# Layer norm up to six tiles ahead, spreads issued in the turning step, six weight pieces behind the MLP's first block, kh ahead of weight copies

## The chip, the core and the metric

The kernel runs on one core of a Trainium2 chip. The metric is the time of one execution on the device in microseconds (us), as the median of several runs. A profiled execution gives the trace: every instruction of the engines PE (TensorE: matmuls and transposes; PEld is its weight load), DVE (VectorE), ACT (ScalarE), POOL (GpSimd) and of SP (SyncE), whose queue issues all DMAs here. Each engine and SP's queue take their instructions strictly in the program's order, so whatever stands behind a waiting instruction on the same engine waits too.

## The reference

Two layers, each of a linear attention block and an MLP, both with a residual, on x of 2048 rows by 448 columns in float32:

```python
x = A_x
x = x + _A_ref(_layernorm(x), A_wqkv, A_wo)     # layer 0
x = x + _B_ref(_layernorm(x), B_w1, B_b1, B_w2, B_b2)
...                                             # the same two lines again: layer 1
def _A_ref(x, wqkv, wo):
    q, k, v = ...                               # x @ wqkv, 16 heads of 28
    pq, pk = phi(q), phi(k)                     # phi(t) = where(t > 0, t + 1, exp(t)) + 1e-6
    kv = einsum("bhsd,bhse->bhde", pk, v)
    z = einsum("bhsd->bhd", pk)
    num = einsum("bhqd,bhde->bhqe", pq, kv)
    den = einsum("bhqd,bhd->bhq", pq, z)[..., None] + 1e-6
    return (num / den) @ wo                     # heads put side by side again
def _B_ref(x, w1, b1, w2, b2):                  # w1: 448 x 1792, w2: 1792 x 448
    return gelu(x @ w1 + b1) @ w2 + b2
```

## The kernel before

The 2048 rows are 16 tiles of 128 rows. A float32 product is made from three matmuls on rounded pieces (hi x hi, hi x lo, lo x hi), so every operand is split: ACT casts the high piece, DVE or POOL subtracts it to get the low one. That holds for activations (`XH`, `XL`), for kh and kl, for the normalized tile (`xnh`, `xnl`), for q's and k's weights, and for w1 and w2.

**Phase 1** (`phase1`, L456) goes over the tiles in steps t = 0 to 15. In step t it does, for tile t: K (PE, 11 matmuls with k's weights into `psk`), kp (ACT and DVE: phi), kh (ACT casts kh, L400, DVE subtracts to kl and adds e to `za`, which becomes z), s (ACT and POOL split the normalized tile), G (PE, 11 matmuls of the *previous* tile's xn with its kh and kl, into the four banks `acc`), Q (PE, 11 matmuls with q's weights; steps 0 to 9 only, six Q blocks are kept as fill for later) and, one step later, qp (phi of q and its store to DRAM). For later tiles it does a (LN statistics: `bn_stats`, `bn_aggr`, an add on DVE, then `rs`, a power on POOL), n (DVE normalizes in place), and tu (DVE turns 32 x 32 squares into `sq`; every second tile the pair is stored to DRAM by SP, L257). sp (SP, four DMAs, L263) reads the pair back spread out, so that it is transposed; X splits it to XH and XL for K. The first six tiles of layer 0 are transposed on PE instead (T, L228, with a small ACT copy `tail` of the last columns). In the source G is thus a tile behind K: PE's order is K(t), T(t+1), G(t-1), Q(t), K(t+1).

The order inside a step is the string `STEP` (L447). Tile t + 4 is normalized in step t, with four exceptions in `FIRST` (L448), and an x tile is loaded two steps ahead of that. Layer 1's tiles 0 to 3 are normalized, turned and spread in the last MLP block of layer 0.

**Weights of the MLP** are staged in 30 pieces (`bg_pieces`, L296): 16 of w1, 14 of w2. `background(n)` (L324) first works off the pieces it asked for last time (ACT casts, POOL subtracts), then asks for n more: SP issues the load into one of two buffers tagged `xn`, so an issue waits until POOL is done with the piece two before. Phase 1 of layer 0 calls it with `BG = 2` in steps 1 to 15, between tu and kh; two more calls after phase 1 work off the rest.

**Between phase 1 and the MLP** stands a list in `ORDER` (L439): the last G, z (PE, then ACT's `zb`, L512), gt (ACT and DVE copy the four banks), kv (PE, L533), the mask, four products with wo (`m`), the first four tiles' output, with the six Q blocks as fill. wv and wo come from `trans_load` (L500), called at t = 14.

**The MLP** runs over four blocks b of 512 rows, in each over 14 columns i of 128 of the 1792: `mlp1` of column i + 1 (11 matmuls into `hp`, ACT's gelu `g` and cast `gh`, DVE's `gl`), work for the next block's attention (`behind`, in the order of the `PLAN` tables), `mlp2` of column i (12 matmuls). SP's DMAs before the first block copy M's pieces to new rows (`trans_chunks`, L565).

The x tiles share nine buffers (`H`), `sq`, `sp`, wv and wo share five (`S`).

Of the kernel before, what the change touches and what calls it, by code (L numbers as in the profile page):

```python
# [22 lines left out]
def linear_attn_mlp_kernel(  # L23
# [15 lines left out]
    S, D = x0.shape  # L39
# [31 lines left out]
    def t512(tag, bufs, name, dt=F32):  # L71
        return work.tile([128, 512], dt, name=name, tag=tag, bufs=bufs)
# [15 lines left out]
    def stage_piece(src, c, eng, s):  # L88

        if c < 3:  # L90
            eng.dma_start(s, src[c * 128:(c + 1) * 128, :])
        else:
            eng.dma_start(s[0:64], src[TL:D, :])
            eng.dma_start(s[64:128], src[TL:D, :])
        return s
# [198 lines left out]


    def bg_pieces():  # L296
        for fc in range(4):
            sl = slice(fc * D, (fc + 1) * D)
            for c in range(4):
                s = stage_piece(w1[:, sl], c, sp, t512("xn", 2, "stg")[:, :D])  # L300

                def go(c=c, s=s, sl=sl):
                    if c < 3:
                        act.copy(w1h[:, c, sl], s)
                        pool.tensor_tensor(w1l[:, c, sl], s, f(w1h[:, c, sl]), op=OP.subtract)
                    else:
                        tmp = t512("e", 3, "bx", F32R)[:, :D]
                        act.copy(tmp, s)
                        act.copy(w1x[0:64, sl], s[0:64])
                        pool.tensor_tensor(w1x[64:128, sl], s[64:128], f(tmp[64:128]), op=OP.subtract)  # L310
                yield go
        for i in range(NF):
            s = t512("xn", 2, "stg")[:, :D]
            sp.dma_start(s, w2[i * 128:(i + 1) * 128, :])

            def go(i=i, s=s):
                act.copy(w2h[:, i], s)
                pool.tensor_tensor(w2l[:, i], s, f(w2h[:, i]), op=OP.subtract)
            yield go
# [4 lines left out]
    def background(n):  # L324
        while bg_wait:
            bg_wait.pop(0)()
        for _ in range(n):
            g = next(bg, None)
            if g is not None:
                bg_wait.append(g)  # L330
# [28 lines left out]
    def stage_sp(l, t):  # L359
        if t >= TURNED[l]:  # L360
            block(("a", l, t // 4))
            spread(("a", l, t // 4), t % 4 // 2)
# [28 lines left out]
        ke[l, t] = phi(o, "ek", o)  # L391

    ke = {}
    BG = 2

    def stage_kh(l, t, za):
        e = ke.pop((l, t))
# [46 lines left out]
    )  # L444
    DEFER = NT - ORDER.split().count("Q")

    STEP = "sp a qp K T X s n G kp tu bg kh Q"  # L447
    FIRST = {0: (2, 3), 1: (4,), 2: (5, 6), 3: (7,)}  # L448
    loaded = {0: 3}

    def load_to(l, t):
        for u in range(loaded.get(l, 0), min(t + 1, NT)):
            load_x(l, u)
        loaded[l] = max(loaded.get(l, 0), min(t + 1, NT))

    def phase1(l, tr):  # L456
        za = consts.tile([128, D], F32, name="za", tag="za")
        acc = [bank("acc", 4, f"G{c}")[:, :D] for c in range(4)]
        for t in range(NT):
            load_to(l, (4 if l == 0 else 5) if t == 0 else t + 6)  # L460
            norm = [u for u in (FIRST.get(t, (t + 4,)) if l == 0 else (t + 4,)) if u < NT]
            for tok in STEP.split():
                if tok == "sp":
                    if (t + 3) % 2 and t + 3 < NT and (l == 0 or t >= 2):
                        stage_sp(l, t + 3)
                elif tok == "a":
                    for u in norm:
                        stage_a(l, u)
                elif tok == "n":
                    for u in norm:  # L470
                        stage_n(l, u)
                elif tok == "tu":
                    for u in norm:
                        stage_t(l, u)
                elif tok == "T" and t + 1 < NT:
                    stage_b(l, t + 1)
                elif tok == "X" and t + 1 < NT and (l == 0 or t + 1 >= 4):
                    stage_x(l, t + 1)
                elif tok == "K":
                    stage_k(l, t)  # L480
                elif tok == "qp":
                    stage_qphi()
                elif tok == "kp":
                    stage_kphi(l, t)
                elif tok == "kh":
                    stage_kh(l, t, za)
                elif tok == "s":
                    stage_s(l, t)
                elif tok == "G" and t >= 1:
                    stage_g(l, t - 1, acc)  # L490
                elif tok == "bg" and l == 0 and t >= 1:
                    background(BG)
                elif tok == "Q" and t < DEFER:
                    stage_q(l, t)
            if t == 14:
                trans_load(l, tr)
        return za, acc


    def trans_load(l, tr):  # L500
        tr.wv = stage_square(wqkv[:, 2 * D:])
        tr.wo = []
        for h in range(2):
            s = half("wot")[:G, :2 * D].rearrange("p (g n) -> p g n", g=2)
            sp.dma_start(s, wo[h * 2 * G:(h + 1) * 2 * G, :].rearrange("(g p) n -> p g n", p=G))
            tr.wo += [s[:, 0], s[:, 1]]
# [73 lines left out]
        sp.dma_start(pqt[l, t], pq_d[l][t * 128:(t + 1) * 128, :])  # L580

    def q_z(l, b, j, tr):
        pz = pzs[l, b, j] = t448(f"W{4 + j % 2}", 1, "pz")
        pool.tensor_tensor(pz, pqt[l, b * 4 + j], tr.zb, op=OP.mult)  # L584

    def q_scale(l, b, j, tr):
# [215 lines left out]
    for l in range(LAYERS):  # L802
        tr = SimpleNamespace(mp={})
        za, acc = phase1(l, tr)
        if l == 0:
            background(99)
            background(0)
        fill = list(range(DEFER, NT))

# [20 lines left out]
        for b in range(NB):  # L830
            acc = [bank("acc", 4, f"y{j}")[:, :D] for j in range(4)]
            nxt = b + 1 < NB
            if not nxt and l + 1 < LAYERS:
                st_k = stage_square(wqkv[:, D:2 * D])
                st_q = stage_square(wqkv[:, :D])
                load_to(l + 1, 3)
            for i in range(NF):
                if i + 1 < NF:
                    mlp1(l, b, i + 1)
                elif nxt:  # L840
                    mlp1(l, b + 1, 0)
                if nxt:
                    behind(l, b, i, tr)
                elif l + 1 < LAYERS:
                    if i == 2:
                        split_kq("k", st_k)
                    if i == 5:
                        split_kq("q", st_q)
                    if i in (3, 4, 6, 7):
                        t = (3, 4, 6, 7).index(i)  # L850
                        stage_a(l + 1, t)
                        stage_n(l + 1, t)
                        stage_t(l + 1, t)
                    if i in (6, 9):
                        stage_sp(l + 1, 1 if i == 6 else 3)
                    if i >= 9 and i < 13:
                        stage_x(l + 1, i - 9)
                mlp2(l, b, i, acc)

# [27 lines left out]
```

## Time and profile before

| what | value |
|---|---|
| time, median of 3 runs (lowest to highest) | 910.58 us (910.14 to 912.22) |
| the profiled execution's own time | 911.72 us |
| its span, first to last instruction | 910.0 us |
| mean granted PE clock | 0.991 |
| idle time of PE before G's first matmul, waiting for kh (L400), five times | 5.2 us |
| idle time of PE before the first kv matmul, waiting for gt | 2.0 us |

In rows in order of time the first number is the start in us from the span's start, the second the length; the engine, line and operation follow, then output<-inputs. A bracket at the end tells how long the engine had been idle and what ended that. In rows of stretches the first pair is the stretch; a number in (x...) counts instructions, those that the edge cuts among them; the last three numbers are the granted PE clock (1.00 is full speed), the DMA engines' busy share and GB/s. Matmuls are pipelined and overlap in the rows, so PE can be shown busy and still be held up. SPq is SP's DMA queue.

### The profile page before, as it was taken

What the parts mean: (1) busy time and instruction counts of PE and PEld (TensorE: products, weight loads), DVE (VectorE), ACT (ScalarE), POOL (GpSimd) and SP (SyncE); (2) the same over time, 40 slices, a digit from 0 to 9 for tenths busy, and PEclk for the clock granted to TensorE, in tenths of its full rate; (3) what the DMA queues carried; (4) which work ended last, traced back from release to release, by engine and by line L of the source; (5) the groups of instructions that cost most, each with busy time, mean ns of one, the idle gap of its engine ahead of it and who ended that gap; (6) DMA issues with size and microseconds to landing.
All of it is one profiled execution on the core that took longest, in us unless ns stands there. A gap on an engine that the chain in (4) does not pass through costs nothing.

```text
span 910.0 us, 11659 instructions
## 1 busy us (share of the span) xinstructions
PE 885.5 (97%) x4184; PEld 777.0 (85%) x4184; DVE 498.1 (55%) x970; ACT 340.0 (37%) x586; POOL 207.2 (23%) x243
## 2 busy tenths in 40 slices
PE   7999879999999999999999999999999999999998
PEld 5899768888888888888889998888888888888887
DVE  5798548645744735225448885865555654433112
ACT  3677633422322332333345554342233132222222
POOL 4466742213113102002013233230220220210000
PEclk8999989999999999999999999999999999999999
DMA  6386460532324231132124436145124134020001
GB/s 172 106 239 207 138 197 28 174 105 90 120 87 132 71 104 47 47 118 78 60 81 152 152 110 184 51 123 162 57 76 165 57 115 136 24 70 15 26 1 41
DMA packets 62762, 93.71 MB, mean 103 GB/s; under 512 B 8816, under 2 KB 57968, under 8 KB 62704
## 3 DMA queue, kind: packets, MB, share of 16 engines
q1 hardware_dynamic: 62704, 92.97, 33.1%
q8 instruction: 33, 0.54, 0.3%
q14 instruction: 25, 0.20, 0.1%
HBM read 55.65 MB, written 34.08 MB: 99 GB/s over the span
## 4 chain that ended last, share of the span: by engine, by line
PE 75%; DVE 7%; issue 1%; ACT 1%; DMA 1%; POOL 0%; SPq 0%; DVEq 0%; POOLq 0%
PE y L699 10%; PE y L701 9%; PE y L700 9%; PE hp L683 8%; PE hp L682 8%; PE hp L681 8%; PE hp L685 3%; PE hp L684 3%; PE op L634 2%; PE op L633 2%; PE op L635 2%; PE psq L279 1%; PE psq L280 1%; PE psq L281 1%; PE G L428 1%
## 5 line engine op out<-in xcount | busy, mean ns | idle before, releaser
L691 DVE TENSOR_TENSOR gl<-g,gh 128x512 fp32r<-128x512 f32 x112 | 78.4, 700 | 311.8 <-ACT gh L690 311.8
L687 ACT ACTIVATE g<-hp,b1s 128x512 f32<-128x512 f32 x112 | 77.1, 688 | 410.7 <-PE hp L685 410.6
L699 PE MATMUL y<-w2h,gh 128*128 128x448 f32 x448 | 163.8, 366 | 0.6 <-DVE x L705 0.6
L701 PE MATMUL y<-w2h,gl 128*128 128x448 f32 x448 | 163.7, 365 | 0.0
L700 PE MATMUL y<-w2l,gh 128*128 128x448 f32 x448 | 163.6, 365 | 0.0
L683 PE MATMUL hp<-XL,w1h 128*128 128x512 f32 x336 | 131.3, 391 | 0.3 <-DVE XL L270 0.3
L681 PE MATMUL hp<-XH,w1h 128*128 128x512 f32 x336 | 131.5, 391 | 0.1
L682 PE MATMUL hp<-XH,w1l 128*128 128x512 f32 x336 | 131.5, 391 | 0.0
L183 POOL TENSOR_TENSOR brs<-bve,mhalf 128x1 f32<-128x1 f32 x64 | 40.1, 627 | 385.2 <-DVE bve L181 379.8
L699 PEld LDWEIGHTS y<-w2h,gh 128*128 128x128 f32 x448 | 84.1, 188 | 10.3 <-issue 1.4
L700 PEld LDWEIGHTS y<-w2l,gh 128*128 128x128 f32 x448 | 84.1, 188 | 8.3
L701 PEld LDWEIGHTS y<-w2h,gl 128*128 128x128 f32 x448 | 84.2, 188 | 6.6
L683 PEld LDWEIGHTS hp<-XL,w1h 128*128 128x128 f32 x336 | 63.1, 188 | 14.7 <-DVE XL L270 1.2
L681 PEld LDWEIGHTS hp<-XH,w1h 128*128 128x128 f32 x336 | 63.1, 188 | 11.7 <-ACT XH L269 0.8
L682 PEld LDWEIGHTS hp<-XH,w1l 128*128 128x128 f32 x336 | 63.1, 188 | 11.3
L690 ACT CAST gh<-g 128x512 fp32r<-128x512 f32 x112 | 69.7, 622 | 3.6
L584 POOL TENSOR_TENSOR pz<-pq,zb 128x448 f32<-128x448 f32 x32 | 37.3, 1174 | 82.0 <-DVE dn L590 46.9
L177 DVE BATCH_NORM_STATS2 bst<-x 128x6 f32<-128x448 f32 x64 | 39.9, 623 | 7.6 <-DMA x<-in_A_x_dram 3.4
L648 POOL TENSOR_TENSOR x<-x,b2b 128x448 f32<-128x448 f32 x32 | 36.8, 1150 | 31.6 <-DVE xm L190 23.3
L684 PE MATMUL hp<-XH,w1x 128*128 128x512 f32 x112 | 43.6, 389 | 0.0
L685 PE MATMUL hp<-XL,w1x 128*128 128x512 f32 x112 | 43.6, 389 | 0.0
L427 PE MATMUL G<-kh,xnh 128*128 128x448 f32 x96 | 37.1, 386 | 5.2 <-ACT kh L400 5.2
(144 smaller groups left out, 1584.2 us busy)
## 6 DMA issues: line engine op xcount, KB each, us to landing
x<-in_A_x_dram SPq DMA_DIRECT2D x32, 224.0 KB, 3.8
pq_d<-eq SPq DMA_DIRECT2D x32, 224.0 KB, 2.3
pq<-pq_d SPq DMA_DIRECT2D x32, 224.0 KB, 3.4
x<-x_d SPq DMA_DIRECT2D x32, 224.0 KB, 3.6
sq_a<-sq SPq DMA_DIRECT2D x13, 512.0 KB, 2.9
sp<-sq_a SPq DMA_DIRECT2D x52, 128.0 KB, 3.1
sq_q<-sq SPq DMA_DIRECT2D x12, 512.0 KB, 2.6
sp<-sq_q SPq DMA_DIRECT2D x48, 128.0 KB, 3.0
```

What stands on the lines that cost most here:

```text
L183: pool.tensor_tensor(rs, ve, mhalf, op=OP.pow)
L681: pe.matmul(o, w1h[:, c, s], x.moving(x.hi, c), start=(c == 0), stop=False)
L682: pe.matmul(o, w1l[:, c, s], x.moving(x.hi, c), start=False, stop=False)
L683: pe.matmul(o, w1h[:, c, s], x.moving(x.lo, c), start=False, stop=False)
L684: pe.matmul(o, w1x[:, s], x.moving(x.hi, 3), start=False, stop=False)
L685: pe.matmul(o, w1x[:, s], x.moving(x.lo, 3), start=False, stop=True)
L687: act.activation(g, hp, AF.Gelu_apprx_tanh, bias=b1s[:, i:i + 1])
L690: act.copy(gh, g)
L691: dve.tensor_sub(gl, g, f(gh))
L699: pe.matmul(acc[j], gh[:, s], w2h[:, i], start=first, stop=False)
L700: pe.matmul(acc[j], gh[:, s], w2l[:, i], start=False, stop=False)
L701: pe.matmul(acc[j], gl[:, s], w2h[:, i], start=False, stop=last)
```

## The change

- LN runs further ahead. `NORM` lists for each layer and step which tiles are normalized; in layer 0 all are done by step 9 (before: step 11), in layer 1 by step 8; some steps take two tiles. Loads follow it. Layer 1's tile 4 joins tiles 0 to 3 in the last MLP block (`PRE`).
- sp is the last token of the step that turns the odd tile, no longer the first of a later one.
- Step 0 has an order of its own, `STEP_0`: kp stands ahead of a, s and kh.
- In all steps kh stands ahead of bg.
- `BG` is a list: two pieces per step in steps 1 to 9, one in steps 10 to 15, 24 in all. The last six go through two other buffers (tags W5 and W6) and are asked for in columns 0 to 5 of the MLP's first block of layer 0, each worked off one column later. So that W5 is free, the blocks after the first use W4 alone for pz.
- wv is loaded after step 11 and wo after step 13 (both after step 14 before).

The lines that this text speaks of:

```diff
+        def stage():
+            nonlocal n
+            n += 1
+            if n <= LATE:
+                return t512("xn", 2, "stg")[:, :D]
+            return t448(f"W{5 + n % 2}", 1, "stg")
...
-    BG = 2
...
-    STEP = "sp a qp K T X s n G kp tu bg kh Q"
-    FIRST = {0: (2, 3), 1: (4,), 2: (5, 6), 3: (7,)}
+    STEP = "a qp K T X s n G kp tu kh bg Q sp"
+    STEP_0 = "K T X kp a s kh n tu G Q bg sp"
+    NORM = (
+        ((2,), (3, 4), (5, 6), (7,), (8,), (9,), (10, 11), (12,), (13, 14), (15,)),
+        ((5,), (6,), (7,), (8,), (9, 10), (11,), (12,), (13, 14), (15,)),
+    )
+    PRE = 5
+    BG = [0] + [2] * 9 + [1] * 6
+    LATE = sum(BG)
...
-            load_to(l, (4 if l == 0 else 5) if t == 0 else t + 6)
-            norm = [u for u in (FIRST.get(t, (t + 4,)) if l == 0 else (t + 4,)) if u < NT]
-            for tok in STEP.split():
+            norm = NORM[l][t] if t < len(NORM[l]) else ()
+            if t + 1 < len(NORM[l]):
+                load_to(l, min(NORM[l][t + 1][-1] + 1, NT - 1))
+            for tok in (STEP if t else STEP_0).split():
                 if tok == "sp":
-                    if (t + 3) % 2 and t + 3 < NT and (l == 0 or t >= 2):
-                        stage_sp(l, t + 3)
+                    for u in norm:
+                        if u % 2:
+                            stage_sp(l, u)
...
-                elif tok == "bg" and l == 0 and t >= 1:
-                    background(BG)
+                elif tok == "bg" and l == 0:
+                    background(BG[t])
...
-            if t == 14:
+            if t == 11:
+                tr.wv = stage_square(wqkv[:, 2 * D:])
+            if t == 13:
                 trans_load(l, tr)
...
-        pz = pzs[l, b, j] = t448(f"W{4 + j % 2}", 1, "pz")
+        pz = pzs[l, b, j] = t448(f"W{4 if b else 4 + j % 2}", 1, "pz")
...
-            background(99)
             background(0)
...
+                if l == 0 and b == 0:
+                    background(1)
```

Three places show the order on an engine. First ACT in layer 0, from the split of tile 12 (`xnh`, the first operation of step 12 here) to the split of tile 13's XH; `ek` and `kh` are phi and the cast of k, `w2h` the cast of a weight piece. Before:

```order
L379 CAST xnh<-x_12_717 128x448
L289 ACTIVATE ek<-psk 128x448
L290 ACTIVATE ek<-ek 128x448
L317 CAST w2h<-stg 128x448 x2
L400 ACTIVATE kh<-psk,tiny 128x448
L269 CAST XH<-sp 128x512
```

And in the changed kernel:

```order
L388 CAST xnh<-x_12_638 128x448
L289 ACTIVATE ek<-psk 128x448
L290 ACTIVATE ek<-ek 128x448
L408 ACTIVATE kh<-psk,tiny 128x448
L326 CAST w2h<-stg 128x448
L269 CAST XH<-sp 128x512
```

kh has moved ahead of the weight casts, and there is one cast instead of two; the next XH still stands behind it.

Second, DVE in layer 0, step 0, from its first instruction after the weights' splits (tile 1's XL is L235; L177 to L181 are a tile's LN statistics, L347 or L356 its normalization, L292 on `psk` is k's phi). Before:

```order
L177 BN_STATS bst<-x_2_92 128x6
L179 BN_AGGR bmv<-bst 128x2
L181 TENSOR_SCALAR bve<-bmv 128x1
L177 BN_STATS bst<-x_3_211 128x6
L179 BN_AGGR bmv<-bst 128x2
L181 TENSOR_SCALAR bve<-bmv 128x1
L235 TENSOR_TENSOR XL<-tp,XH 128x512
L347 TENSOR_SCALAR x_2_92<-x_2_92,bmv,brs 128x448
L347 TENSOR_SCALAR x_3_211<-x_3_211,bmv,brs 128x448
L292 SCALAR_TENSOR_TENSOR psk<-psk,ek 128x448
L401 SCALAR_TENSOR_TENSOR kl<-psk,kh 128x448
L403 COPY za<-psk 128x448
```

And in the changed kernel:

```order
L235 TENSOR_TENSOR XL<-tp,XH 128x512
L292 SCALAR_TENSOR_TENSOR psk<-psk,ek 128x448
L177 BN_STATS bst<-x_2_92 128x6
L179 BN_AGGR bmv<-bst 128x2
L181 TENSOR_SCALAR bve<-bmv 128x1
L409 SCALAR_TENSOR_TENSOR kl<-psk,kh 128x448
L411 COPY za<-psk 128x448
L356 TENSOR_SCALAR x_2_92<-x_2_92,bmv,brs 128x448
```

XL and psk now come first, tile 3 has moved out of the step, and tile 2's normalization stands behind kl and za.

Third, SP's queue at the end of phase 1 in layer 0. L257 stores the last pair of turned tiles, L263 spreads it, L314 or L323 loads a piece of w2, L114 to L118 load wv, L505 or L523 load wo. Before:

```order
L257 DMA sq_a_3_1_1165<-sq 128x1024
L314 DMA stg<-in_B_w_dram 128x448 x2
L263 DMA sp<-sq_a_3_1_1165 32x4x256 x4
L314 DMA stg<-in_B_w_dram 128x448 x6
L114 DMA stg<-in_A_wqkv_dram 128x2x448
L116 DMA stg<-in_A_wqkv_dram 128x448
L117 DMA stg<-in_A_wqkv_dram 64x448
L118 DMA stg<-in_A_wqkv_dram 64x448
L505 DMA wot<-in_A_wo_dram 112x2x448 x2
L314 DMA stg<-in_B_w_dram 128x448 x2
```

And in the changed kernel:

```order
L257 DMA sq_a_3_1_1052<-sq 128x1024
L323 DMA stg<-in_B_w_dram 128x448 x2
L263 DMA sp<-sq_a_3_1_1052 32x4x256 x4
L427 DMA pq_d_71<-eq 128x448
L323 DMA stg<-in_B_w_dram 128x448 x2
L114 DMA stg<-in_A_wqkv_dram 128x2x448
L116 DMA stg<-in_A_wqkv_dram 128x448
L117 DMA stg<-in_A_wqkv_dram 64x448
L118 DMA stg<-in_A_wqkv_dram 64x448
L323 DMA stg<-in_B_w_dram 128x448 x2
L523 DMA wot<-in_A_wo_dram 112x2x448 x2
L323 DMA stg<-in_B_w_dram 128x448 x2
```

Ten pieces were loaded after the last store, six of them in a row ahead of wv; now there are eight, two at a time: ahead of the spread, ahead of wv, between wv and wo, and behind wo. (L427 is the store of the last eq, which stood further up.)

More of the change, by code (lines that the diff above doesn't have):

```diff
@@ L296, in bg_pieces @@
     def bg_pieces():
+        n = 0
+        def stage():
[4 more added lines that the diff above has]
+            return t448(f"W{5 + n % 2}", 1, "stg")
         for fc in range(4):
@@ L299, in bg_pieces @@
             for c in range(4):
-                s = stage_piece(w1[:, sl], c, sp, t512("xn", 2, "stg")[:, :D])
+                s = stage_piece(w1[:, sl], c, sp, stage())
                 def go(c=c, s=s, sl=sl):
@@ L312, in bg_pieces @@
         for i in range(NF):
-            s = t512("xn", 2, "stg")[:, :D]
+            s = stage()
             sp.dma_start(s, w2[i * 128:(i + 1) * 128, :])
@@ L445, in linear_attn_mlp_kernel @@
     DEFER = NT - ORDER.split().count("Q")
-    STEP = "sp a qp K T X s n G kp tu bg kh Q"
-    FIRST = {0: (2, 3), 1: (4,), 2: (5, 6), 3: (7,)}
+    STEP = "a qp K T X s n G kp tu kh bg Q sp"
[7 more added lines that the diff above has]
+    LATE = sum(BG)
     loaded = {0: 3}
     def load_to(l, t):
-        for u in range(loaded.get(l, 0), min(t + 1, NT)):
+        for u in range(loaded.get(l, 0), t + 1):
             load_x(l, u)
-        loaded[l] = max(loaded.get(l, 0), min(t + 1, NT))
+        loaded[l] = max(loaded.get(l, 0), t + 1)
     def phase1(l, tr):
@@ L500, in trans_load @@
     def trans_load(l, tr):
-        tr.wv = stage_square(wqkv[:, 2 * D:])
         tr.wo = []
@@ L835, in linear_attn_mlp_kernel @@
                 st_q = stage_square(wqkv[:, :D])
-                load_to(l + 1, 3)
+                load_to(l + 1, PRE - 1)
             for i in range(NF):
@@ L848, in linear_attn_mlp_kernel @@
                         split_kq("q", st_q)
-                    if i in (3, 4, 6, 7):
-                        t = (3, 4, 6, 7).index(i)
+                    if i in (3, 4, 6, 7, 8):
+                        t = (3, 4, 6, 7, 8).index(i)
                         stage_a(l + 1, t)
@@ L853, in linear_attn_mlp_kernel @@
                         stage_t(l + 1, t)
-                    if i in (6, 9):
-                        stage_sp(l + 1, 1 if i == 6 else 3)
-                    if i >= 9 and i < 13:
+                        if t % 2:
+                            stage_sp(l + 1, t)
+                    if 9 <= i < 13:
                         stage_x(l + 1, i - 9)
```

## The prediction

> **What bounds the kernel now.** I read the page's first part, then the busy times by stretch, then the rows in order of time where a stretch loses something. On the page, engine PE (TensorE's matmuls) is busy almost all the time:
> ```profile
> PE 885.5 (97%) x4184; PEld 777.0 (85%) x4184; DVE 498.1 (55%) x970; ACT 340.0 (37%) x586; POOL 207.2 (23%) x243
> ```
> So only PE's lost time can be won. The next view cuts the span where PE changes its work; the columns are length, then each engine's busy time (and instructions), the granted PE clock, DMA share and GB/s.
> ```profile
> 17.41:36.77 19.36, 15.54 (x76) 13.20 (x75) 14.09 (x31) 9.16 (x20) 7.19 (x11) 1.00 0.19 62
> 69.00:92.00 23.00, 23.00 (x115) 21.32 (x114) 19.40 (x41) 17.15 (x34) 15.12 (x18) 1.00 0.71 211
> 92.09:118.28 26.19, 23.54 (x98) 19.06 (x97) 12.40 (x21) 16.12 (x31) 19.36 (x21) 0.93 0.51 150
> 120.12:161.85 41.73, 36.43 (x189) 30.86 (x188) 29.96 (x62) 14.15 (x27) 13.53 (x14) 0.96 0.30 93
> 466.65:482.02 15.37, 13.85 (x59) 12.16 (x58) 11.03 (x24) 6.58 (x11) 3.89 (x6) 0.89 0.47 162
> 482.02:547.60 65.58, 65.58 (x324) 60.57 (x323) 55.03 (x107) 38.65 (x71) 21.85 (x31) 1.00 0.45 141
> 547.60:566.17 18.57, 17.48 (x82) 14.97 (x82) 9.69 (x15) 8.24 (x16) 5.15 (x8) 1.00 0.72 186
> 566.17:601.38 35.21, 34.26 (x189) 29.50 (x189) 29.13 (x62) 13.31 (x25) 11.87 (x12) 1.00 0.14 50
> ```
> Row 482.02 has PE busy throughout: 65.58 over 324 is 0.2024 us per matmul. Matmuls overlap, so a stretch's loss is its length less its count times that, not its idle time.
> - Layer 0, steps 0 to 2 (17.41): 66 matmuls of 448 columns (76 less 8 transposes at about 0.11 and two cut by the edge) need 14.2; lost 5.1.
> - Layer 0, steps 10 to 15 (92.09): 97 x 0.2024 = 19.6; lost 6.6.
> - The stage between phase 1 and the MLP holds the same 189 instructions in both layers: 41.73 in layer 0, 35.21 in layer 1; lost 6.5.
> - Layer 1, start (466.65): 58 x 0.2024 = 11.7; lost 3.6.
> - Layer 1, last steps (547.60): 81 x 0.2024 = 16.4; lost 2.2.
>
> Together 24.0 us: the most that this change can win. Part of it is a halved clock, seen in equal stretches of 3.41 us (first and second of each pair adjacent):
> ```profile
> 111.45:114.87 3.42, 1.75 (x7) 1.00 0.27 72
> 114.87:118.28 3.41, 3.41 (x10) 0.50 0.90 297
> 473.27:476.68 3.41, 1.89 (x9) 1.00 0.00 0
> 476.68:480.09 3.41, 3.41 (x11) 0.50 0.17 67
> 22.71:26.12 3.41, 1.87 (x8) 1.00 0.00 0
> 26.12:29.53 3.41, 3.41 (x19) 1.00 0.43 133
> ```
> A stretch with PE busy for 1.75 or 1.89 us was followed by one at 0.50, which costs 1.7; one with 1.87 was not. About 1.5 us of idle time in one such stretch is the edge. The kv stage holds a third (its clock is 0.96 over 41.73). The Trainium skill ("TensorE: Matmul & The Clock Gate", section on HAM oscillation) lets the clock fall only after a PE gap of over some 3.4 us; these rows contradict it. By that rule the forecast below would be 897.8.
>
> **Kh ahead of the weight copies; one piece per step; six pieces later (layer 0, steps 10 to 15).** In order of time, ACT, the PE matmul behind it, and the same pattern after phase 1:
> ```profile
> 112.38 0.56 ACT L317 CAST w2h<-stg 128x448 fp32r<-128x448 f32 x1 [2.29 <-DMA stg<-in_B_w_dram]
> 112.85 0.63 ACT L400 ACTIVATE kh<-psk,tiny 128x448 fp32r<-128x448 f32 x1
> 113.53 0.47 PE L427 MATMUL G<-kh,xnh 128*128 128x448 f32 x1 [1.49 <-ACT kh L400]
> 125.34 1.12 ACT L317 CAST w2h<-stg 128x448 fp32r<-128x448 f32 x2 [7.48 <-DMA stg<-in_B_w_dram]
> 127.47 0.45 PE L533 MATMUL kvp<-gt,stg 128*112 128x112 f32 x2 [1.99 <-ACT gt L523]
> ```
> ACT waits for a weight's DMA, kh stands behind it, PE behind kh. The DMA is late because of SP's queue:
> ```profile
> 101.10 13.42 SPq L314 DMA_DIRECT2D stg<-in_B_w_dram  x6
> 114.57 0.43 SPq L114 DMA_DIRECT2D stg<-in_A_wqkv_dram  x1
> 117.88 1.04 SPq L314 DMA_DIRECT2D stg<-in_B_w_dram  x2
> ```
> Six issues crawl for 13.42 us, each waiting for one of two buffers; wv and wo wait behind them, and the last two pieces behind those. Afterwards kh waits only for psk, and a late copy holds only the next XH, which PE wants a K block and a G block later (22 matmuls, 4.5 us). With LN done by step 9, DVE drops out too. I leave 0.3 for kl and take 0.4 for step 8 (below): **-5.9**; bounds -4.0 (copies still hold XH once or twice) and -6.5.
>
> **The kv stage.** With one piece per step, wv at step 11 and wo at step 13, the last two copies still stand ahead of zb on ACT, but their DMAs are issued one step apart instead of after 13.42 us of crawl. PE has G(14), a Q block, zp and G(15) to do meanwhile, over 33 matmuls or 6.7 us. Layer 1, without copies, is the nearest row: 35.21. I take nearly all of the 6.5: **-6.3**; bounds -4.5 and -6.5.
>
> **Six pieces behind the MLP's first block.** The price is not the six casts (ACT idles 3.60 per column below) but the first one's wait:
> ```profile
> x<-in_A_x_dram SPq DMA_DIRECT2D x32, 224.0 KB, 3.8
> ```
> That is the page's median landing time for a load of a piece's size; then in order of time:
> ```profile
> 175.71 0.59 SPq L565 DMA_DIRECT2D wq<-Ml  x1
> 176.95 0.69 ACT L687 ACTIVATE g<-hp,b1s 128x512 f32<-128x512 f32 x1 [3.60 <-PE hp L685]
> 181.89 0.69 ACT L687 ACTIVATE g<-hp,b1s 128x512 f32<-128x512 f32 x1 [3.60 <-PE hp L685]
> ```
> The first piece's DMA comes behind the 14 chunk copies, so it is issued at 176.3 in these times and lands near 180. Its cast stands ahead of the g of 176.95, which would start near 180.5; g and gh take ACT 1.34 (4.94 per column less 3.60), to 181.9, gl follows. PE uses gh from about 181.8, when its next hp is done. **+0.4**, between 0 and 1.5. Later pieces are issued a column (4.94) or more ahead. SP's spread of sq_q moves by some 2 us; its reader comes two columns later. POOL's pz now waits for DVE's read of the one buffer, which comes just before it anyway: nothing.
>
> **Layer 0, steps 0 to 2.** What PE waited for:
> ```profile
> 17.06 0.63 DVE L177 BATCH_NORM_STATS2 bst<-x 128x6 f32<-128x448 f32 x1
> 18.01 0.62 DVE L177 BATCH_NORM_STATS2 bst<-x 128x6 f32<-128x448 f32 x1
> 18.95 0.68 DVE L235 TENSOR_TENSOR XL<-tp,XH 128x512 fp32r<-128x512 f32 x1
> 19.55 1.63 DVE L347 TENSOR_SCALAR x<-x,bmv,brs 128x448 f32<-128x448 f32 x2
> 19.69 0.47 PE L281 MATMUL psk<-wk,XL 128*128 128x448 f32 x1 [1.52 <-DVE XL L235]
> 22.65 0.63 DVE L292 SCALAR_TENSOR_TENSOR psk<-psk,ek 128x448 f32<-128x448 f32 x1 [1.48 <-ACT ek L290]
> 24.07 0.47 PE L427 MATMUL G<-kh,xnh 128*128 128x448 f32 x1 [1.82 <-ACT kh L400]
> ```
> Two tiles' statistics (0.95 each, 18.01 to 18.95) stood ahead of XL and psk. Now XL and psk go first: from 17.06, XL 0.68, psk 0.63, one tile's statistics 0.95, kl and za like psk about 0.6 each, normalizing 0.8 (half of 1.63), and a small ACT copy, some 0.3, end near 21.6. Only then can PE transpose tile 2. It was through K(1) nine matmuls after the wait at 19.69; without that wait (1.52 and some 0.16 of overlap) this is 19.69 - 1.68 + 1.8 = 19.8. So 1.8 is lost there (a halved clock after it, 1.7 more, is in the bound), but G then finds kh ready. Steps 1 and 2 norm two tiles each, so DVE stays behind: adding up the same durations, I find 0.4 at G(1)'s kl and 1.0 at the Q block whose bank eq must free first. 3.2 of 5.1 stays: **-1.9**; bounds -0.5 and -4.0.
>
> **Two tiles in one step** (layer 0 steps 6 and 8, layer 1 steps 4 and 7). DVE's groups between 40 and 90 us:
> ```profile
> L347 DVE TENSOR_SCALAR x<-x,bmv,brs 128x448 f32<-128x448 f32 x8 | 9.0, 1129 | 0.0
> L251 DVE STREAM_TRANSPOSE sq<-x 128x384 f32<-128x384 f32 x8 | 4.5, 564 | 0.0
> ```
> A step with Q is 33 matmuls, 6.7 us; DVE is busy 19.40 of 23.00 there, 5.6 per step. One more tile adds 0.95 + 1.13 + 0.56 + some 0.3 = 2.9, so 8.5: 1.8 over. But G(t) comes 6.7 after K(t) and the chain from ek to kl needs about 3.1 (1.3 from psk's start to kh's end in layer 1's rows below, and three more instructions of 0.6), so DVE may run late by 1.8 once; between steps 6 and 8 it regains only about one. I take 0 at step 6 and the 0.4 above at step 8. Spreads, SP and loads: a spread in the turning step only moves ahead of one x load, and that tile is needed a step later.
>
> **Layer 1, start and end.**
> ```profile
> 470.61 0.63 DVE L177 BATCH_NORM_STATS2 bst<-x 128x6 f32<-128x448 f32 x1 [3.14 <-DMA x<-x_d]
> 473.49 0.62 DVE L292 SCALAR_TENSOR_TENSOR psk<-psk,ek 128x448 f32<-128x448 f32 x1
> 472.31 1.01 POOL L380 TENSOR_TENSOR xnl<-x,xnh 128x384 fp32r<-128x384 f32 x1
> 474.83 0.47 PE L427 MATMUL G<-kh,xnh 128*128 128x448 f32 x1 [1.33 <-ACT kh L400]
> ```
> psk will now go before the new tile, at about 471.6, so kh is ready when PE ends K(1) (474.83 - 1.33 - 0.16 = 473.34). What is late next: on POOL, xnl of tile 0 stands behind the rs of the new tile. Here xnl ended 2.7 after that tile's statistics began (470.61 to 473.32); begun at 472.2, behind psk, that is 474.9, where PE wants it at 473.75, with G's third matmul. 1.3 with its overlap stays and, being under 1.5, most likely brings no halved clock: **-2.3**; bounds -0.8 and -3.6. At the end the spreads leave steps earlier and 0.3 stays: **-1.9**; bounds -1.0 and -2.2.
>
> **The rivals.**
> - *DVE sets the pace in the two-tile steps.* If no slack hides them, 4 x 1.8 = 7.2 comes back: 899.9. For it: DVE's 19.40 of 23.00. Against: the row at 482.02, where it is busy 55.03 of 65.58 and PE never waits. 0.07.
> - *The halved clock has another cause than these stalls.* Then three half-clock stretches stay, 3 x 1.7 = 5.1: 897.8. Against it: each fall comes right after a stretch that was half idle. 0.05. This is what the Trainium skill's rule above would give.
> - *zb still waits for the last two copies*, so the change does not do this part: the kv stage keeps its 6.3: 899.0. 0.07.
> - *Slower: casts hold ACT in the MLP block.* If each of the six waited the 7.48 seen at 125.34, a column would take ACT 7.48 + 0.56 + 1.34 (its busy time per column, 4.94 - 3.60) = 9.4 instead of 4.94; six times 4.4, less a slack of 3.5 (gh ends near 178.3, 1.34 after g's start, and is needed at 181.8), is 23: about 915. It decides against the change from 6.7 of wait per cast. Against it: SP has nothing of that length queued there. 0.09, of which 0.03 ends within 0.2%.
>
> **How the numbers follow.** -5.9 - 6.3 + 0.4 - 1.9 - 2.3 - 1.9 = -17.9. The profiled execution took 911.72, 1.72 around a span of 910.0, and lies 1.14 over the median of the runs, 910.58. From its own time the sum gives 893.8; from the median, which I predict, 892.7. The ends of all terms give gains of 22.8 and 9.3, so 887.8 to 901.3, which takes in the three mild rivals. Forecast 0.72. A measurement of this kernel tells about 0.2% (1.8 us) from no change: faster 0.91, same 0.03, slower 0.06.
>
> **What would show it.** Right: no PE wait for kh after 40 us; the stage from zp to the first hp near 35.4 in layer 0; the clock at half only around the start. Wrong step by step: PE waiting for the tp transpose by far more than 1.7 near 20 us; for kl in steps 6 or 8; for y's gh in the MLP's first columns; for xnl at layer 1's first G by over 1.3. The forecast as a whole falls if steps 10 to 15 still take more than 4.5 each.

## The result, and the profile after

The changed kernel takes 896.01 us (median of 4 runs, 895.77 to 896.46) against 911.4 for the kernel before beside it. That is 15.4 us less; the ratio is 0.9829 (95% interval 0.9808 to 0.985). 892.7 was forecast, with a range of 887.8 to 901.3. Of the 3.3 us between forecast and result, 0.8 is the kernel before itself: its median was 910.58 when the forecast was made and is 911.4 with one more run. The profiled execution spans 894.7 (before 910.0). The page's first part:

```profile
PE 878.8 (98%) x4184; PEld 772.8 (86%) x4184; DVE 502.3 (56%) x970; ACT 339.5 (38%) x586; POOL 209.1 (23%) x243
```

PE issues the same 4184 instructions in the same order in both kernels, so a stage can be cut at the start of the *same* matmul in both. Here are the stretches of the kernel before, cut that way at K(12), zp, the first and sixth hp, the first y of block 1 and K(2) and K(13) of layer 1 (length, then each engine's busy time and instructions, granted clock, DMA share, GB/s):

```profile
93.51:120.12 26.61, 23.96 (x100) 19.45 (x99) 12.19 (x21) 15.12 (x29) 18.21 (x20) 0.94 0.54 154
161.85:184.12 22.27, 22.27 (x105) 19.34 (x103) 12.77 (x26) 8.96 (x13) 4.99 (x4) 1.00 0.62 191
184.12:246.21 62.09, 61.58 (x286) 53.20 (x285) 35.14 (x72) 17.53 (x29) 11.70 (x12) 1.00 0.27 88
481.41:548.43 67.02, 67.02 (x331) 61.90 (x330) 56.41 (x110) 39.08 (x71) 22.64 (x32) 1.00 0.45 142
```

And of the changed one:

```profile
91.61:111.68 20.07, 20.07 (x101) 18.60 (x100) 12.19 (x18) 13.95 (x27) 13.93 (x17) 1.00 0.64 188
111.68:147.34 35.66, 34.44 (x189) 29.40 (x188) 29.88 (x62) 13.32 (x25) 12.43 (x13) 1.00 0.18 62
147.34:170.40 23.06, 22.54 (x104) 19.26 (x103) 11.83 (x22) 10.46 (x16) 7.69 (x7) 1.00 0.67 209
170.40:233.09 62.69, 61.64 (x286) 53.20 (x285) 39.24 (x76) 19.55 (x33) 17.00 (x16) 1.00 0.33 103
453.53:465.95 12.42, 11.76 (x57) 10.25 (x55) 7.97 (x17) 5.99 (x10) 3.90 (x6) 1.00 0.48 169
465.95:534.15 68.20, 68.20 (x332) 61.94 (x330) 55.47 (x109) 39.76 (x73) 21.59 (x31) 1.00 0.52 166
534.15:550.06 15.91, 15.91 (x78) 14.45 (x77) 9.37 (x13) 8.16 (x15) 4.78 (x6) 1.00 0.32 100
550.06:585.50 35.44, 34.41 (x189) 29.42 (x188) 29.70 (x62) 13.31 (x25) 11.48 (x12) 1.00 0.14 48
```

From K(12) to zp PE no longer stops at all: 20.07 busy of 20.07. The stage after it is down to layer 1's length. Here are the rows on which the argument rests from the changed kernel's view of what PE waits for (total, times, longest):

```profile
PE psk L279 <- ACT XH L234: 3.1, 1, 3.1
PE y L717 <- ACT g L705: 1.7, 2, 0.9
PE tp L228 <- DVE x L356: 1.2, 1, 1.2
PE G L437 <- POOL xnl L389: 0.7, 1, 0.7
PE y L719 <- DVE gl L709: 0.5, 1, 0.5
PE psq L279 <- DVE eq L292: 0.5, 1, 0.5
PE G L436 <- DVE kl L409: 0.4, 1, 0.4
```

No row for kh is left, the kv stage (zp to the first hp) is within 0.3 of the foretold 35.4, and the clock is at half only around the start and at the very end, as the prediction wanted it. Its last sign was a limit of 4.5 for each of steps 10 to 15: they take 4.46, but for step 11 with 4.72. The next table has the stage lengths of all the kernels that the argument needs, cut at the same matmuls (us, each the difference of two starts in the profile). "Weights alone" and the like are experiments below.

| kernel | Q(1) to K(12) | K(12) to zp | zp to 1st hp | 1st to 6th hp | to block 1's y | layer 1: K(0) to K(2) | K(2) to K(13) | K(13) to zp |
|---|---|---|---|---|---|---|---|---|
| before | 66.65 | 26.61 | 41.73 | 22.27 | 62.09 | 14.76 | 67.02 | 17.76 |
| changed | 67.66 | 20.06 | 35.67 | 23.06 | 62.69 | 12.42 | 68.20 | 15.91 |
| changed, again | 66.96 | 20.06 | 35.72 | 23.37 | 62.67 | 12.34 | 66.88 | 15.61 |
| kh alone | 66.66 | 26.76 | 43.76 | 22.27 | 62.11 | 13.26 | 67.03 | 18.41 |
| weights alone | 67.60 | 28.47 | 35.84 | 24.10 | 62.68 | 13.32 | 67.02 | 21.98 |
| weights, wv late | 66.64 | 22.92 | 39.39 | 23.33 | 62.83 | 13.23 | 68.15 | 17.29 |
| layer norm alone | 68.26 | 22.16 | 42.16 | 22.26 | 62.10 | 12.41 | 68.20 | 15.91 |
| best | 66.72 | 20.06 | 35.76 | 22.27 | 62.10 | 11.49 | 68.20 | 15.91 |

By this table and the 2.9 won before Q(1) (26.86 to 23.95), the 15.3 us between the two spans are: -2.9, +1.0, -6.5, -6.1, +0.8, +0.6, -2.3, +1.2, -1.9, and +0.8 in the rest. Three of these stages held a half-clock stretch in the kernel before's trace (K(12) to zp, the kv stage, layer 1's K(0) to K(2)) and hold none now, so about 5 of the 15.3 are clock and the others are waits.

### The profile page after: what moved, and what is told of

The parts are those of the page before. It is cut to its first block, busy times and chain, and to the rows that moved or that the text cites. A ratio compares the mean times of both kernels' runs of the same rounds, so it can differ in the third digit from the quotient of the medians.

```text
span 894.7 us, 11665 instructions
## 1 busy us (share of the span) xinstructions
PE 878.8 (98%) x4184; PEld 772.8 (86%) x4184; DVE 502.3 (56%) x970; ACT 339.5 (38%) x586; POOL 209.1 (23%) x243
## 4 chain that ended last, share of the span: by engine, by line
PE 84%; DVE 7%; issue 2%; DMA 2%; ACT 2%; POOL 2%; SPq 1%; POOLq 0%; DVEq 0%; ACTq 0%
PE y L719 10%; PE y L717 10%; PE y L718 10%; PE hp L701 8%; PE hp L700 8%; PE hp L699 8%; PE hp L703 3%; PE hp L702 3%; PE G L436 2%; PE G L437 2%; PE G L435 2%; PE op L652 2%; PE op L651 2%; PE op L653 2%; PE psk L281 2%
## 5 line engine op out<-in xcount | busy, mean ns | idle before, releaser
L177 DVE BATCH_NORM_STATS2 bst<-x 128x6 f32<-128x448 f32 x64 | 39.8, 622 | 6.3 <-DMA x<-in_A_x_dram 5.2
L389 POOL TENSOR_TENSOR xnl<-x,xnh 128x384 fp32r<-128x384 f32 x32 | 35.4, 1107 | 29.6 <-ACT xnh L388 23.0
```

The source lines that it names most:

```text
L177: dve.bn_stats(st, xs)
```

## The experiments

**Theory:** steps 10 to 15 and the kv stage are won by the weights' part (copies no longer hold kh and zb), and the ends of phase 1 by the layer norm's order. **Rivals:** the layer norm and the spreads did it; the half clock has a cause of its own.

**The copies back ahead of kh** (a_bgkh).

```diff
-    STEP = "a qp K T X s n G kp tu kh bg Q sp"
+    STEP = "a qp K T X s n G kp tu bg kh Q sp"
```

> The changed kernel with the weight copies put back ahead of kh (896.0 is its own time). Theory: the order matters only where a copy waits for its DMA; with one piece a step from step 10 on, each DMA is issued a whole step (about 5 us) before its copy, so kh is held by a copy's own 0.6 us at most and steps 10 to 15 lose 0 to 1 us: 896 to 897. Rival, that kh's place is what won steps 10 to 15: PE waits for kh in most of the six steps, some 0.7 to 1.5 us each, 4 us or more: 900 or more.

Measured 896.18, ratio 0.9829 (0.9815 to 0.9842): as the changed kernel. K(12) to zp took 20.41, against 20.06. Kh's place is worth nothing here.

**The old timetable of the pieces** (a_two).

```diff
-    BG = [0] + [2] * 9 + [1] * 6
+    BG = [0] + [2] * 15
-            if t == 11:
-                tr.wv = stage_square(wqkv[:, 2 * D:])
-            if t == 13:
+            if t == 14:
+                tr.wv = stage_square(wqkv[:, 2 * D:])
```

> The changed kernel with the weights' old timetable: two pieces in every step from 1 to 15, none behind the MLP, wv and wo at step 14; kh stays ahead of the copies. Theory: zb stands behind the last copies on ACT again, so the stage from zp to the first hp goes back from 35.7 to about 41.7 (+6); steps 10 to 15 keep most of their 6.5, since kh no longer stands behind a copy that waits (+0 to +2); the first y column gives its 0.8 back: 901 to 903.5. Rival, that the layer norm done early is what freed these stages: within 2 us of 896.

Measured 904.88, ratio 0.9923 (0.991 to 0.9935): 1.4 above the expected range. K(12) to zp gave back 2.0 (22.02); the kv stage went to 43.81. ACT in this kernel, in order of time, and the stage:

```profile
120.80 1.18 ACT L326 CAST w2h<-stg 128x448 fp32r<-128x448 f32 x2 [6.43 <-DMA stg<-in_B_w_dram]
121.89 0.63 ACT L529 ACTIVATE zb<-zp,zc 128x448 f32<-128x448 f32 x1
```
```profile
113.45:157.26 43.81, 37.35 (x189) 31.74 (x189) 29.88 (x62) 14.69 (x28) 15.56 (x16) 0.92 0.35 114
```

Two copies wait 6.43 for their DMA and zb stands behind them: the predicted cover. The clock of 0.92 is two stretches at half, where the kernel before had one; that is 1.7 of the 2.1 over the expected 6.

**Kh alone, and the weights' part alone, on the kernel before** (b_kh, b_weights). The first swaps `bg` and `kh` in the old `STEP`; the second:

```diff
-    BG = 2
+    BG = [0] + [2] * 9 + [1] * 6
+    LATE = sum(BG)
-    STEP = "sp a qp K T X s n G kp tu bg kh Q"
+    STEP = "sp a qp K T X s n G kp tu kh bg Q"
+            if t == 11:
+                tr.wv = stage_square(wqkv[:, 2 * D:])
-            if t == 14:
+            if t == 13:
                 trans_load(l, tr)
...
```

(also the late pieces, their buffers and pz as in the change.)

> The kernel before with one edit, kh ahead of the weight copies. Putting the copies back ahead in the changed kernel cost nothing. Theory: either of the two edits, kh's place or one piece a step, takes PE's wait out of steps 10 to 15; here kh's place alone does, as the pieces still come two a step: 3 to 5 of the 6.5 us there are won (with the half clock that follows that stall), the stage after them keeps its 41.7: about 907 to 908.5. Rival, that kh's place is worth nothing anywhere and the layer norm's or the pieces' timetable did it: within 1 us of the kernel before.

> The kernel before with the weights' part alone: one piece a step from step 10, six pieces behind the MLP's first block, wv and wo earlier, kh ahead of the copies, pz as changed; the layer norm's order and the spreads stay as they were. Theory: steps 10 to 15 (6.5) and the stage to the first hp (6.0) come from this part, and it pays 0.8 at the first y column and 0.55 twice at the hand-over of the blocks: 911.4 - 12.5 + 1.9 = 901. Rival, that steps 10 to 15 also need the layer norm done by step 9, since DVE is busy with it there: 2 to 4 of the 6.5 stay, 903 to 905.

Both theories failed, and the rivals' times did not come either. Kh alone: 914.73, ratio 1.0022 (1.0009 to 1.0034), slightly slower than before. The weights alone: 913.01, ratio 1.0003 (0.9992 to 1.0013), so a part that was to win 10 us wins nothing. With kh ahead, the wait moves on to XH, the next instruction behind the copies. ACT and PE of the kernel with kh alone:

```profile
102.53 0.57 ACT L317 CAST w2h<-stg 128x448 fp32r<-128x448 f32 x1 [1.15 <-DMA stg<-in_B_w_dram]
105.54 0.62 ACT L269 CAST XH<-sp 128x512 fp32r<-128x512 f32 x1 [2.44 <-DMA sp<-sq_a]
106.21 0.47 PE L279 MATMUL psk<-wk,XH 128*128 128x448 f32 x1 [2.13 <-ACT XH L269]
```

The copies are done at 103.10; what XH then waits for is its own spread, which SP issues behind the last store and two pieces. So XH would be late even with no copy ahead of it. With the weights alone this is worse, and seen best in layer 1, which has no copies: SP's queue, ACT, and the stretch from K(13) to zp.

```profile
544.04 0.43 SPq L114 DMA_DIRECT2D stg<-in_A_wqkv_dram  x1
546.72 2.38 SPq L263 DMA_DIRECT2D sp<-sq_a  x4
554.98 0.62 ACT L269 CAST XH<-sp 128x512 fp32r<-128x512 f32 x1 [7.53 <-DMA sp<-sq_a]
```
```profile
546.46:568.44 21.98, 17.42 (x79) 15.44 (x77) 8.87 (x14) 8.33 (x15) 4.36 (x6) 0.92 0.58 153
```

At step 11 wv's loads go out in front of the last spread, which is only issued in step 12; XH, and so PE, waits for it. Behind wv this spread lands 6.1 to 6.7 us after its issue; in the next experiment, ahead of wv, 2.5 to 2.9. That is +4.2 in layer 1, of which 1.7 is a half-clock stretch, where the prediction had seen only a gain in issuing wv earlier. In layer 0 K(12) to zp is 28.47, with two half-clock stretches in it. Only the kv stage behaves as foretold (35.84).

**New theory:** steps 10 to 15 are freed by tiles that are normalized, turned and spread early; the weights' part frees the kv stage alone, and only where the spreads are out before wv.

**The weights alone with wv at step 14** (b_wlate; wv and wo at step 14 again, the last edit of the diff above undone).

> The weights' part alone once more, but with wv and wo at step 14 as in the kernel before. In the first run of this part XH of step 13 waited 5.89 in layer 0 and 7.53 in layer 1 for a spread issued right behind wv. Theory: wv at step 11 without early spreads was what undid the gain: layer 1's last steps go back from 21.98 to 17.8 (-4.2) and layer 0's steps 10 to 15 from 28.47 to 24 or so (-4), while the stage to the first hp keeps most of its 35.84 (up to +2): 905 to 907. Rival, that the layer norm's work on DVE holds layer 0's steps 10 to 15: layer 1 gives its 4.2 back, but layer 0's steps stay above 26: 908 to 909.

Measured 907.56, ratio 0.9962 (0.9949 to 0.9975), 0.6 above the expected range. Here are K(12) to zp and the stage after it:

```profile
93.50:116.42 22.92, 21.80 (x101) 18.27 (x100) 13.35 (x21) 13.37 (x26) 13.02 (x15) 1.00 0.54 161
116.42:155.80 39.38, 36.07 (x189) 30.20 (x188) 29.75 (x62) 13.57 (x26) 12.53 (x13) 0.96 0.24 80
```

Both layers' ends come back (22.92, and 17.29 in layer 1): wv ahead of the spread was the cause. But 22.92 is also 3.7 less than the kernel before's 26.61, though the layer norm is untouched, and that speaks against the new theory's second half. Kh is ahead in both kernels, "kh alone" with two pieces a step (26.76) and this one with one piece from step 10 (22.92). So the slower pieces do free much of these steps, as long as wv comes late; 1.7 of the 3.7 is the half-clock stretch that this trace does not have there. The price stands in the second row: with wv late, the last copies are late too (the one ahead of zb waits 4.03 for its DMA), and the kv stage keeps only 2.3 of its 6.

**The layer norm's part alone** (b_ln): the change without the weights' edits.

> The kernel before with the layer norm's part alone: tiles up to six ahead, spreads in the turning step, step 0's own order; the weights' timetable, their place ahead of kh, and pz stay as before. The weights' part alone won nothing, since XH of step 13 waited 5.89 for a spread that stood behind wv; so the two parts need each other. Theory: it is the spreads' being early that frees steps 10 to 15, and with it 4 to 5 of the 6.5 come even with two pieces a step, beside 2.9 at the start and 4.3 in layer 1; the stage to the first hp keeps its loss or grows by up to 3, as with the old timetable above (904.9): 903 to 906. Rival, that kh behind the copies brings its waits back: 908 to 910.

Measured 902.98, ratio 0.9896 (0.9875 to 0.9917): the theory, at the near end of its range. K(12) to zp:

```profile
92.24:114.40 22.16, 21.17 (x100) 18.11 (x98) 11.58 (x17) 15.75 (x30) 18.03 (x19) 1.00 0.47 139
```

4.4 of the 6.5 come with two pieces a step and kh *behind* the copies. The gains at the start (Q(1) at 23.98 instead of 26.86) and at layer 1's start and end (12.41 and 15.91) come whole. The kv stage stays at 42.16.

**Layer 0's spreads at their old place, layer norm ahead** (a_nosp).

```diff
-    STEP = "a qp K T X s n G kp tu kh bg Q sp"
+    STEP = "sp0 a qp K T X s n G kp tu kh bg Q sp1"
...
+                if tok == "sp0":
+                    if l == 0 and (t + 3) % 2 and t + 3 < NT:
+                        stage_sp(l, t + 3)
```

> The changed kernel with layer 0's spreads at their old place, at the head of the step two ahead of use, while the layer norm stays ahead. Theory: what the weights' part lacked when alone is the early spread, not DVE's free time: wv, issued at step 11, stands ahead of the last spread, XH waits for it some 5, and PE loses 3 to 6 in steps 10 to 15: 899 to 902. Rival, that the layer norm's work on DVE was what mattered: within 1 us of 896.

Measured 897.18, ratio 0.9829 (0.9808 to 0.9851); in the trace K(12) to zp takes 21.57, 1.5 more. The time lies between the theory and its rival. The expected 3 to 6 did not come, so the late spread by itself is a small part: with tile 15 normalized and stored early, XH waits only 1.49 for the spread behind wv. SP's queue shows why. Here are the last store and XH in this kernel, then the last store with the weights alone:

```profile
81.95 0.33 SPq L257 DMA_DIRECT2D sq_a<-sq  x1
99.70 0.62 ACT L269 CAST XH<-sp 128x512 fp32r<-128x512 f32 x1 [1.49 <-DMA sp<-sq_a]
```
```profile
97.96 0.32 SPq L257 DMA_DIRECT2D sq_a<-sq  x1
```

The store of the last turned pair goes out 9.2 us before K(12) starts (91.15) here, and 3.4 after it (94.58) with the weights alone, where wv and the spread then stand behind the store. What counts is that the tile is turned early. Whether DVE's or POOL's share of that work matters more is not told apart.

**Step 0 of layer 1 in the old order** (a_s1).

```diff
-            for tok in (STEP if t else STEP_0).split():
+            for tok in (STEP if t or l else STEP_0).split():
```

> The changed kernel with step 0 of layer 1 in the order of the other steps, so that the new tile's statistics stand ahead of psk on DVE again. Theory: PE waits for kh about 1.3 us in place of 0.7 for xnl, and as it then idles over 1.5 us in one stretch of 3.41 us, a stretch at half clock follows: +0.7 + 1.7 = +2.3, 898.3 or so. Rival 1, that the half clock has another cause: the stall alone, +0.7, clock 1.00 throughout. Rival 2, that the tile normed earlier (five instead of four before the layer) did it: no change.

Measured 895.83, ratio 0.9827 (0.9813 to 0.984): no difference that the timing tells, 2.5 under the theory. The trace has the stall, at K(0) to K(2) in 13.46 instead of 12.42, but no half clock:

```profile
462.13 0.47 PE L435 MATMUL G<-kh,xnh 128*128 128x448 f32 x1 [1.59 <-ACT kh L408]
```
```profile
457.82:461.24 3.42, 2.72 (x14) 2.18 (x12) 2.53 (x5) 0.72 (x2) 1.96 (x3) 1.00 0.25 78
461.24:464.65 3.41, 2.33 (x10) 1.93 (x11) 3.31 (x9) 3.12 (x6) 0.30 (x1) 1.00 0.37 154
```

The stall of 1.59 lies across an edge of the 3.41 grid (461.24), and neither stretch is half idle. So this run confirms the stall and leaves the half clock open; the next one tests it.

**24 stalls made on purpose** (a_stall).

```diff
+    EXTRA = {(l, b, i): 7 + (l * 12 + b * 3 + k) % 6
+             for l in range(LAYERS) for b in range(4) for k, i in enumerate((3, 7, 11))}
...
+        for _ in range(EXTRA.get((l, b, i), 0)):
+            act.copy(g, g)
```

> The changed kernel with ACT held up on purpose: in columns 3, 7 and 11 of each MLP block, 7 to 12 copies of g onto itself stand between g and gh, so that PE waits 24 times, by some 0.5 to 3.5 us, at many phases of the 3.41 us grid on which the clock is granted. Theory: the next stretch of the grid runs at 0.50 where PE was busy for under about 1.9 us of one stretch; so stalls over 2.5 us nearly always bring it, those under 1.3 never, those between do when they lie whole in one stretch and not when an edge cuts them. Rival, the rule that only a gap of over some 3.4 us does: no half clock for any stall under 3.4.

One run, 1001.9. Stretches of the grid, with a stall of 1.70 whole in one, and one of 1.70 cut by an edge:

```profile
385.55:388.96 3.41, 1.66 (x7) 0.80 (x6) 0.87 (x2) 3.28 (x6) 0.00 (x0) 1.00 0.00 0
388.96:392.38 3.42, 3.42 (x10) 3.07 (x11) 1.98 (x4) 0.33 (x1) 1.14 (x1) 0.50 0.38 153
...
716.64:720.05 3.41, 1.64 (x8) 1.02 (x6) 0.00 (x0) 3.22 (x7) 0.00 (x0) 1.00 0.66 173
...
870.23:873.65 3.42, 2.48 (x11) 1.69 (x10) 0.00 (x0) 3.26 (x6) 0.00 (x0) 1.00 0.00 0
873.65:877.06 3.41, 2.60 (x11) 2.10 (x12) 2.63 (x5) 1.89 (x4) 1.15 (x1) 1.00 0.01 2
```

All 13 stalls of 3.0 or more brought a half clock, three of the four of 2.35, one of the two of 1.70, and the one of 1.05 did not; the other four were under 1.0. The Trainium skill's rule ("TensorE: Matmul & The Clock Gate", HAM oscillation: only gaps of over some 3.4 us) would allow none of the seven from 1.70 to 3.15; the trace has them. The theory's own limit is not exact: after 716.64 (busy 1.64, a stall of 2.35 cut by the edge) the clock stayed at 1.00.

**Pz in two buffers** (a_pz).

```diff
-        pz = pzs[l, b, j] = t448(f"W{4 if b else 4 + j % 2}", 1, "pz")
+        pz = pzs[l, b, j] = t448(f"W{4 if (l, b) == (0, 1) else 4 + j % 2}", 1, "pz")
```

> The changed kernel with pz in two buffers again, except for layer 0's block 1. Theory: with one buffer POOL's pz starts just when DVE has read the last one and runs beside DVE's scale (1.18 in place of 0.63), which delays the adds of x and the y start of the next block by 0.55 where MLP block 0 hands over to block 1, in each layer. With two buffers the scale takes 0.63 in all blocks but the first of layer 0, and layer 1's 0.55 comes back: 895.4; layer 0's hand-over keeps its loss only if block 1's pz is the one that collides, else 894.9. Rival, that the longer scale is hidden: 896.0.

Measured 894.98, ratio 0.9815 (0.9802 to 0.9829): 1.0 less, as the theory, though its runs spread over 2 us. The trace is firmer: from the sixth hp to block 1's y 62.13 instead of 62.69, and from layer 1's first hp to the end 308.61 instead of 309.25. The last scale before the hand-over to block 1 in the kernel before, then POOL and DVE of the changed one:

```profile
244.13 0.63 DVE L595 SCALAR_TENSOR_TENSOR pq<-pq,rd 128x448 f32<-128x448 f32 x1
```
```profile
230.01 1.15 POOL L602 TENSOR_TENSOR pz<-pq,zb 128x448 f32<-128x448 f32 x1 [3.38 <-DVE dn L608]
230.46 1.18 DVE L613 SCALAR_TENSOR_TENSOR pq<-pq,rd 128x448 f32<-128x448 f32 x1
```

With one buffer pz starts when DVE has read the last one, and the scale that follows takes 1.18 beside it. The Trainium skill ("SBUF — State Buffer", two separate sides) says that a DVE operation with two SBUF inputs and a GpSimd operation that reads SBUF contend for one pair of ports, which the first of them locks for its whole instruction. The row agrees roughly: held until pz's end at 231.16 and then taking its 0.63, the scale would end at 231.79, and it ends at 231.64.

**The changed kernel again** (a_same).

> The changed kernel once more, unaltered, beside the next kernels and with its own profile. Theory: the stretch from 462.23 to 549.85 in its first profile, where 425 matmuls follow each other at 206.7 ns in place of 202.7 and 1.7 us go without any wait, is chance and not the change: the four runs above show it nowhere at that length, so it is absent here too; 896.0 within 0.8. Rival, that the change brings it: it stands again between 460 and 550.

Measured 895.92, ratio 0.9812 (0.9797 to 0.9828); layer 1 from K(2) to K(13):

```profile
465.59:532.47 66.88, 66.88 (x331) 61.97 (x330) 55.21 (x109) 39.36 (x73) 22.90 (x31) 1.00 0.54 169
```

66.88 instead of 68.20 for the same matmuls, in the same kernel: the change does not always bring it. It is not rare either: the layer norm alone, a_nosp and the best kernel have it (68.20), and so has b_wlate (68.15), in which the layer norm is untouched.

**Four repairs** (best): pz as in a_pz, and

```diff
+    STEP_1 = "K T X kp s a kh n tu G Q bg sp"
-         ... (10, 11), (12,), (13, 14), (15,)),
+         ... (10, 11), (12,), (13,), (14,), (15,)),
-            for tok in (STEP if t else STEP_0).split():
+            for tok in (STEP if t else STEP_1 if l else STEP_0).split():
-                if l == 0 and b == 0:
+                if l == 0 and b == 0 and i != 1:
                     background(1)
```

> The changed kernel with four edits where its trace still shows losses: pz in two buffers except in layer 0's block 1 (1.0 less, as measured alone); in layer 1's step 0 xnl ahead of the new tile's rs on POOL (PE's 0.66 at G); the first late piece copied a column later (0.8 at the first y); no second two-tile step at step 8 (0.7 at kl). Theory: 896.0 - 3.2 = 892.8. Rival, that these small waits only move to the next cover: 894 to 895.

Measured 892.57 (891.55 to 893.21), ratio 0.9783 (0.9761 to 0.9805): it beats both kernels, by 3.4 under the changed one's 896.01. Its stretches from the first to the sixth hp and on to block 1's y:

```profile
146.89:169.15 22.26, 22.26 (x104) 19.34 (x103) 12.58 (x26) 9.99 (x15) 6.80 (x6) 1.00 0.66 207
169.15:231.25 62.10, 61.60 (x286) 53.20 (x285) 36.73 (x72) 19.50 (x33) 17.31 (x17) 1.00 0.36 104
```

Both are back at the lengths of the kernel before.

## Why the prediction was right, and where it was not

- **Steps 10 to 15, -5.9:** the changed trace shows -6.5 and then +1.0 between Q(1) and K(12), -5.5 together (in the second profile -6.5 and +0.3). The size was right and the cause only in part. The prediction gave the gain to kh's place and the slower pieces, with "DVE drops out too" as an aside. Kh's place is worth nothing in either kernel. The slower pieces, with kh ahead and wv late, win 3.7; the layer norm done early wins 4.4 alone; both together win the 6.5. And the edits that the term named, with wv at step 11 as in the change, lose 1.9 by themselves (1.7 of it a second half-clock stretch), so the right size owes something to luck: the layer norm's part, which the term counted as an aside, was needed to get it. The prediction had even written down what happens ("a late copy holds only the next XH, which PE wants a K block and a G block later"), but gave XH a slack that it has only when its spread is early. The stretch cut at 92.09 also has the wrong name: K(12) starts at 93.51, so all of this loss lay in steps 12 to 15 and the Q block behind them; steps 10 and 11 (84.59 to 93.51, 44 matmuls in 8.92) lost nothing.
- **The kv stage, -6.3:** -6.1. Cause and size right: zb behind the last two copies (a_two brings the loss back, the weights alone take it away). What it needs was missed: wv before them on SP, and that in turn needs early spreads. Wv at step 11 and wo at step 13 were costed as free; without the layer norm's part they cost 4.2 in layer 1, and in layer 0 K(12) to zp is 28.47 with them and 22.92 without.
- **Six pieces behind the MLP's first block, +0.4:** +0.8 (1.1 in the second profile, and up to 1.8 in others with the same code). The copy waited for its DMA until about the foretold place, but the term left out that POOL, held up by its half of the copy, would then do pz beside DVE's gl. ACT, POOL and DVE in the changed kernel, in order of time:

```profile
164.76 0.57 ACT L326 CAST w2h<-stg 128x448 fp32r<-128x448 f32 x1 [5.92 <-DMA stg<-in_B_w_dram]
```
```profile
166.51 1.16 POOL L602 TENSOR_TENSOR pz<-pq,zb 128x448 f32<-128x448 f32 x1
```
```profile
166.60 1.62 DVE L709 TENSOR_TENSOR gl<-g,gh 128x512 fp32r<-128x512 f32 x1 [4.54 <-ACT gh L708]
```

- **Pz's one buffer, "nothing":** +0.6 in each layer. The step asked whether the buffer is free in time, not what POOL's new start runs beside.
- **Layer 0, steps 0 to 2, -1.9:** -2.9 up to Q(1), -2.7 over the prediction's own stretch (19.4 to 16.7). The order of the waits was right (1.2 at the tp transpose where 1.8 was foretold, 0.5 at eq for 1.0); each was sized too long, and the 0.4 at G(1)'s kl did not come.
- **Two tiles in one step:** PE waits 0.4 for the kl made in step 8, as predicted, and that block takes 2.9 instead of 2.2; it waits for nothing at step 6. The second profile of the same kernel has no wait for kl, so the 0.4 is not in every execution.
- **Layer 1's start, -2.3, and end, -1.9:** -2.3 and -1.9. Xnl was late next, as foretold, by 0.7 and not 1.3. But 1.5 of the kernel before's 14.76 there went with a half-clock stretch in its trace: three kernels with the same code at this place (kh alone, both with the weights alone) took 13.2 to 13.3 without one. Against these the gain is 0.9.
- **Missed altogether:** +1.2 in layer 1's steps, which the second profile does not have and whose cause is open.
- **The rivals:** DVE as the pace of two-tile steps and casts that hold ACT did not come true. Zb waits for no copy now; it waits 1.80 for PE's zp. The half clock has these stalls as its cause (a_stall), but whether one brings it depends on the grid.

The sum was -17.9; the traces give -15.3. The 2.6 between them are the steps from Q(1) to zp (0.4), the kv stage (0.2), the first MLP block (0.4), pz (1.2), the slow steps of layer 1 (1.2) and 0.2 in the rest, less the 1.0 that the first steps won beyond their term.

## What to carry to other kernels

A wait on an in-order engine is cured for the instruction that was moved, and passes to the next one behind it unless that one's input is early too: follow the queue two instructions further before giving an edit its price. A part of a change that wins nothing alone can pay beside another: the weights' part alone gave 913.01, and beside the layer norm's part (902.98) it brings the time to 896.01. So test each part on the kernel before as well as undoing it in the new one, and compare each result with every earlier one: the layer norm alone and the slower pieces with a late wv each won most of the same 6.5. When a buffer is taken away, ask not only whether it is free in time but what the delayed instruction will now run beside.

## What the chip showed unexpectedly

- Half clock: stalls of 1.33 us and more brought a stretch of 3.41 us at 0.50 (1.7 us lost) where they lay whole in one stretch of the grid, in all cases but one, a stall of 1.51 (at 128.88 with the layer norm alone); stalls of 1.6 to 1.85 cut by an edge did not. Behind the start, what counts is PE's idle time in one full-speed stretch: with 1.67 us or more the next stretch was at half in every trace kept here, but for one (1.77 idle, at 716.64 in the run with 24 stalls); of five with 1.51 to 1.59 one was (1.52). So the limit lies near 1.6, a little over the prediction's 1.5, and is not sharp. The grid lies differently in each execution (an edge at 8.36 us in one profile of the changed kernel, at 9.14 in the other), so a profile of one execution shows such a loss or misses it.
- Two paces of PE: the same stage of layer 1 takes 66.88 or 68.20 us, with no wait and the clock at 1.00 in both; the 330 matmuls that start in it follow each other at 202.7 and 206.7 ns on average (66.88 and 68.20 over 330). One kernel showed both in two executions. What starts it stays open.
- Beside POOL's pz, DVE's operations with two inputs took 1.18 for 0.63 (the scale) and 1.62 for 0.69 (gl, beside two of POOL's in turn).
